# The last chunk of a mixture of experts: which engine adds products 1, 2 and 5 to the results

## The chip, the cores and the metric

The kernel runs on one core of one Trainium2 chip. The core's engines work side by side, each through its own queue in order, and wait for each other by semaphores: TensorE multiplies matrices into PSUM, VectorE and ScalarE work on tensors elementwise and can read PSUM, GpSimd works elementwise on SBUF, and SyncE (SP) issues DMAs, as ScalarE and GpSimd can too. The metric is the device time of one execution in microseconds (us). A profile is one further execution, recorded instruction by instruction.

## The reference

Two stages follow each other. The first is attention with two kinds of heads (4 batches, 8 heads, 768 positions, head size 64); its output is laid out as x with 3072 tokens of 512 values. The second is a mixture of 8 experts in which every expert works on every token:

```
logits = x @ w_gate
P = exp(logits - max);  8 times: P /= row sums, P /= column sums, P *= N / E
for e in range(8):
    h = max(x @ w1[e], 0)          # 3072 x 1024
    ye = h @ w2[e]                 # 3072 x 512
    out += P[:, e:e+1] * ye
```

Only the last `h @ w2[e]` and its weighted sum into `out` are touched here.

## The kernel before

The attention and the first expert come first and are not touched. Then a list `works` holds all pairs (e, c): experts 1 to 7, and for each the six chunks c of 512 tokens. The last pair is (7, 5).

Each of the two matrix products of a chunk is made by a scheme of the Strassen kind, with seven products of half-size blocks in place of eight and sums of blocks before and after. `left` and `right` (L611, L620) make the sums of input blocks on VectorE: two of the seven left factors of the second layer are plain blocks of h that serve products 1 and 2, one is a plain block for product 4, and four are sums. `combine_h` (L644) makes these four, in the order X[0] to X[3]: product 5 takes X[0], product 6 takes X[1] (which needs X[0]), product 7 takes X[2], and product 3 takes X[3] (which needs X[1]). Each is a sum over 128x1024 16-bit values at L617.

`layer2` (L734) multiplies. Its products accumulate in PSUM, in three groups called y, z and w, so that a product is added to what its bank already holds: y collects products 1, 6, 7, 4, w collects 5 and 3, z has product 2 alone. After each product the bank's present content belongs to one block (i, n) of the results, so it is read at once, and the next product of that group waits for the reader. `steps` (L771) lists group and block of each:

```
1: ("y", True, False, (0, 0)), 2: ("z", True, True, (0, 0)), 5: ("w", True, False, (1, 1)),
6: ("y", False, False, (0, 1)), 3: ("w", False, True, (0, 1)),
7: ("y", False, False, (1, 1)), 4: ("y", False, True, (1, 0)),
```

Each product has two halves q of 128x256. In the last chunk (`final`) each half has a PSUM bank of its own, so that TensorE can fill one while the other is read; in all other chunks both halves share a bank.

`add` (L754) reads the bank and adds it, times the token's weight for the expert (a column of Pne), to the result tile `acc[c]`. There are two ways. VectorE does it in one instruction per half (scalar_tensor_tensor, L764). Or ScalarE makes a scaled copy of both halves in a tile named add (L761, three buffers), and GpSimd issues a DMA that adds the tile to `acc[c]`, which lies in SBUF (L769). Products 2, 3 and 4 go the second way in all chunks but the last two, where VectorE adds everything. A block is stored (`store`, L727) when its last product of expert 7 has been added: block (0, 0) after products 1 and 2, (1, 1) after 5 and 7, (0, 1) after 6 and 3, (1, 0) after 4 alone. For the last chunk one half of each store is issued by SP and the other by ScalarE's queue.

What sets the order: `body` (L792) runs one pair, and in its seven slots interleaves the first layer of the next chunk with the second layer of the one before. After the last pair a loop runs the second layer of the last chunk alone, with the two remaining sums of h between its first steps (L822 to L824). VectorE's instructions stand in just the order in which this code issues them, as the whole loop is under a manual schedule for VectorE. The order on the other engines is left to a scheduler, which keeps the dependences and may move matmuls of one product between those of another. In the kernel before TensorE's order in the last chunk is 1, 5, 2 (but for one matmul), 6, the rest of 2, 3, 7, 4. VectorE's is: sums X[0], X[1], X[2], both adds of product 1, sum X[3], and then the adds of 5, 6, 2, 7, 3 and 4.

Of the kernel before, what the change touches and what calls it, by code (L numbers as in the profile page):

```python
# [14 lines left out]
ALU = mybir.AluOpType  # L15
# [17 lines left out]
def kernel(  # L33
# [13 lines left out]
    nc = tc.nc  # L47
# [28 lines left out]
    acc = [xp.tile([128, 2, 2, 2, 256], F32, tag=f"acc{c}", name=f"acc{c}") for c in range(NB // 4)]  # L76
# [79 lines left out]
    def round_first(h0):  # L156
# [9 lines left out]
        out=ret_u,  # L166
# [20 lines left out]
        out=retf, in_=ret_u.rearrange("p (e two) -> p e two", two=2)[:, :, 0]  # L187
# [140 lines left out]
    def first_steps(b, g):  # L328
# [18 lines left out]
        def layer2(sb):  # L347
# [10 lines left out]
            return 2  # L358

        return [partial(layer1, i) for i in range(4)], [partial(layer2, sb) for sb in range(2)]  # L360

    fillers = []
# [8 lines left out]
    with tc.manual_schedule(engines={mybir.EngineType.Pool}):  # L371
        nc.gpsimd.affine_select(
            out=ident16, in_=ident16, compare_op=ALU.is_equal, fill=0.0,
            base=0, pattern=[[-1, 128]], channel_multiplier=1,
        )
        for o in range(2):
# [3 lines left out]
                out=f4, in_=f4, compare_op=ALU.is_ge, fill=0.0,  # L380
# [4 lines left out]
                out=w4, in_=w4, compare_op=ALU.is_ge, fill=0.0,  # L385
# [187 lines left out]
    for it in range(8):  # L573
# [3 lines left out]
            out=Pne, in0=Pne, in1=rr.unsqueeze(2).broadcast_to([128, NB, E]), op=ALU.mult  # L577
        )
        nc.vector.tensor_reduce(
            out=bs, in_=Pne.transpose([0, 2, 1]), axis=AX.X, op=ALU.add  # L580
# [5 lines left out]
        if it == 7:  # L586
            nc.vector.tensor_scalar(
                out=rcs, in0=rcs, scalar1=float(NTOK) / E, scalar2=None, op0=ALU.mult
            )
        nc.vector.tensor_tensor(  # L590
            out=Pne, in0=Pne, in1=rcs.unsqueeze(1).broadcast_to([128, NB, E]), op=ALU.mult
# [16 lines left out]
    works = [(e, c) for e in range(1, E) for c in range(NCH)]  # L608
# [118 lines left out]
    def store(c, i, n):  # L727
        for o in range(2):
            (nc.scalar if c == NCH - 1 and o else nc.sync).dma_start(
                out=out[ts(c, CH), :].rearrange("(q i p c) (n d) -> i n c p q d", q=2, i=2, c=2, n=2)[i, n, o],  # L730
                in_=acc[c][64 * o:64 * o + 64, i, n, :, :],
            )

    def layer2(e, c):  # L734
        banks = {}
        final = (e, c) == works[-1]

        def product(k, bank, first, last=False):
            if first and final:
                banks[bank] = [psB.tile([128, 512], F32, tag="l1" if bank == "y" else "l2",  # L740
                                        name=f"l2{bank}{q}")[:, 0:256] for q in range(2)]
            elif first:
                t = psB.tile([128, 2, 256], F32, tag="l2", name=f"l2{bank}")
                banks[bank] = [t[:, q, :] for q in range(2)]
            for q in range(2):
                for f in range(4):
                    nc.tensor.matmul(  # L747
                        out=banks[bank][q], lhsT=lefts2[e, c][k - 1][:, q, f, :],
                        rhs=rights2[e][k - 1][:, f, :],
                        start=(first and (final or q == 0) and f == 0),  # L750
                        stop=(last and (final or q == 1) and f == 3), skip_group_check=True,
                    )

        def add(bank, i, n, by_dma):  # L754
            if by_dma:
                t = mp.tile([128, 2, 256], F32, tag="add", bufs=3, name="add")
            for q in range(2):
                dst = acc[c][:, i, n, q, :]
                w = Pne[:, 4 * c + 2 * q + i, e:e + 1]
                if by_dma:  # L760
                    nc.scalar.activation(out=t[:, q, :], in_=banks[bank][q], func=AF.Copy,  # L761
                                         bias=0.0, scale=w)
                else:
                    nc.vector.scalar_tensor_tensor(  # L764
                        out=dst, in0=banks[bank][q], scalar=w, in1=dst,
                        op0=ALU.mult, op1=ALU.add,
                    )
            if by_dma:
                nc.gpsimd.dma_start(out=acc[c][:, i, n, :, :], in_=t, accum_op=ALU.add)  # L769

        steps = {  # L771
            1: ("y", True, False, (0, 0)), 2: ("z", True, True, (0, 0)), 5: ("w", True, False, (1, 1)),
            6: ("y", False, False, (0, 1)), 3: ("w", False, True, (0, 1)),
            7: ("y", False, False, (1, 1)), 4: ("y", False, True, (1, 0)),
        }
        done = {}
        for k in (1, 5, 6, 2, 7, 3, 4):
            bank, first, last, (i, n) = steps[k]
            product(k, bank, first, last)
            add(bank, i, n, k in (2, 3, 4) and (e, c) not in works[-2:])  # L780
            done[i, n] = done.get((i, n), 0) + 1
            if e == E - 1 and done[i, n] == (1 if (i, n) == (1, 0) else 2):
                store(c, i, n)
            yield
# [7 lines left out]
    def body(n):  # L792
        e, c = works[n]
        if c == 0 and e + 1 < E:
            expw[e + 1] = load_expert(e + 1)
        if c == 2 and e + 1 < E:
            gens["w"] = combine_w(e + 1)
        if e == 1:
            gens["first"] = weight_first(c)
            gens["x"] = combine_x((c + 1) % NCH)  # L800
        for slot in range(7):
            go("l1", 2 if n == 0 and slot == 0 else 1)
            if slot in (1, 3):
                go("w")
                go("x", 2)
            go("l2")
            if slot in (2, 3, 5, 6):
                go("first")
            if slot in (2, 3):
                go("h")  # L810
            if n == 0 and slot == 0:
                run(combine_w(1), 9)
        gens["h"] = combine_h(e, c)
        go("h", 2)
        gens["l2"] = layer2(e, c)
        if n + 1 < len(works):
            gens["l1"] = layer1(*works[n + 1])
# [41 lines left out]
```

## Time and profile before

| | us |
|---|---|
| median of 6 runs | 706.03 |
| lowest and highest run | 705.28 and 706.4 |
| the profiled execution | 705.86 |
| its span from first to last recorded instruction | 704.1 |
| TensorE at work in the span | 686.2 |
| VectorE | 569.3 |
| ScalarE | 416.9 |
| GpSimd | 151.4 |
| first matmul of the last chunk's second layer | at 690.02 |
| last add of VectorE starts, lasts | at 698.64, 0.48 |

The program ends shortly after the span. In the tables below, times are counted from the span's start; a row such as `L764 DVE ... acc_84<-l2y_10647,Pne,acc_84` is an instruction of line 764 on VectorE (DVE) that writes acc_84, the results of the last chunk, and reads the PSUM bank of one half of group y. PE is TensorE, PEld its weight load, ACT ScalarE, POOL GpSimd, SP SyncE.

### The profile page before, as it was taken

The page shows a single profiled execution, that of the slowest core. Times are in us where ns is not written, and L with a number is a line of the kernel's source. Part 1 is how long each engine was busy: PE and PEld are TensorE (multiplying, and loading weights), DVE is VectorE, ACT ScalarE, POOL GpSimd, SP SyncE. Part 2 cuts the span into 40 slices and gives each one's busy share as a digit, 9 for nine tenths or more (in the row PEclk, how much of TensorE's full clock was granted, in tenths as well). Part 3 has the DMA queues.
Part 4 walks back from the last instruction along what each step waited for, and adds up shares of the span by engine and source line. Part 5 has one row for each costly group of instructions (what it writes and reads, how often), then busy time and mean ns, then how long its engine had stood idle before and what let it go on. Part 6 is the DMA issues. An engine that isn't in the chain of part 4 may idle for free.

```text
span 704.1 us, 17055 instructions
## 1 busy us (share of the span) xinstructions
PE 686.2 (97%) x6932; PEld 570.0 (81%) x6932; DVE 569.3 (81%) x1158; ACT 416.9 (59%) x779; POOL 151.4 (22%) x183
## 2 busy tenths in 40 slices
PE   7999999999999999999999999999999999999995
PEld 3666666666588888888888888888888888888884
DVE  6775765757889978898888879887888889877786
ACT  6787676774885555555555555555655555555550
POOL 7431220000012131212212121222212121121210
PEclk8999999999999999999999999999999999999999
DMA  9999591000734287346924694359424954345774
GB/s 179 180 191 129 47 79 15 2 1 3 118 61 76 47 133 122 62 75 110 145 48 77 95 145 76 61 82 163 84 48 76 151 90 76 61 76 111 149 160 122
DMA packets 84223, 65.61 MB, mean 93 GB/s; under 512 B 48304, under 2 KB 64688, under 8 KB 84144
## 3 DMA queue, kind: packets, MB, share of 16 engines
q0 software_dynamic: 74976, 57.17, 58.6%
q1 hardware_dynamic: 7536, 6.30, 3.6%
q10 hardware_dynamic: 1632, 1.05, 0.5%
q8 instruction: 54, 0.88, 0.5%
q14 instruction: 25, 0.20, 0.1%
HBM read 52.45 MB, written 6.29 MB: 83 GB/s over the span
## 4 chain that ended last, share of the span: by engine, by line
PE 61%; DVE 1%; issue 0%; ACT 0%; DVEq 0%
PE l1y L679 17%; PE l2y L747 17%; PE l1w L679 9%; PE l2w L747 9%; PE l2z L747 4%; PE l1z L679 4%; DVE acc_84 L764 1%; DVE S_7_5_10640 L617 0%; DVE S_7_5_10643 L617 0%; DVE S_7_5_10642 L617 0%; DVE acc_83 L764 0%; ACT R_4602 L688 0%; DVEq L854 0%; DVE S_7_5_10641 L617 0%
## 5 line engine op out<-in xcount | busy, mean ns | idle before, releaser
L761 ACT ACTIVATE add<-l2w,Pne 128x256 f32<-128x256 f32 x80 | 33.7, 473 | 66.3 <-PE l2w L747 64.1
L761 ACT ACTIVATE add<-l2y,Pne 128x256 f32<-128x256 f32 x80 | 33.8, 474 | 11.0 <-PE l2y L747 10.0
L761 ACT ACTIVATE add<-l2z,Pne 128x256 f32<-128x256 f32 x80 | 33.7, 473 | 8.7 <-PE l2z L747 8.7
L337 PEld LDWEIGHTS <-w_0_126 128*128 128x128 f16 x384 | 35.4, 98 | 4.1 <-issue 0.2
L769 POOL DMA_DIRECT2D acc_79<-add x21 | 17.7, 844 | 78.8 <-ACT add L761 57.7
L769 POOL DMA_DIRECT2D acc_82<-add x21 | 17.8, 847 | 68.0 <-ACT add L761 68.0
L769 POOL DMA_DIRECT2D acc_81<-add x21 | 17.7, 844 | 68.0 <-ACT add L761 68.0
L769 POOL DMA_DIRECT2D acc_80<-add x21 | 17.7, 845 | 67.9 <-ACT add L761 67.9
L769 POOL DMA_DIRECT2D acc_83<-add x18 | 15.1, 841 | 54.7 <-ACT add L761 46.8
L769 POOL DMA_DIRECT2D acc_84<-add x18 | 15.4, 854 | 44.5 <-ACT add L761 44.0
L764 DVE SCALAR_TENSOR_TENSOR acc_79<-l2y,Pne,acc_79 128x256 f32<-128x256 f32 x42 | 18.3, 477 | 7.2 <-PE l2y L747 7.1
L764 DVE SCALAR_TENSOR_TENSOR acc_83<-l2y,Pne,acc_83 128x256 f32<-128x256 f32 x44 | 19.1, 477 | 3.2 <-PE l2y L747 3.2
L764 DVE SCALAR_TENSOR_TENSOR acc_80<-l2y,Pne,acc_80 128x256 f32<-128x256 f32 x42 | 18.3, 477 | 4.1 <-PE l2y L747 4.1
L764 DVE SCALAR_TENSOR_TENSOR acc_82<-l2y,Pne,acc_82 128x256 f32<-128x256 f32 x42 | 18.3, 477 | 4.1 <-PE l2y L747 4.1
L764 DVE SCALAR_TENSOR_TENSOR acc_81<-l2y,Pne,acc_81 128x256 f32<-128x256 f32 x42 | 18.3, 477 | 4.1 <-PE l2y L747 4.1
L764 DVE SCALAR_TENSOR_TENSOR acc_84<-l2y,Pne,acc_84 128x256 f32<-128x256 f32 x36 | 15.7, 477 | 7.1 <-PE l2y L747 7.1
L679 PEld LDWEIGHTS <-S_2_3734 128*128 128x128 f16 x192 | 18.8, 98 | 2.7 <-issue 0.5
L679 PEld LDWEIGHTS <-S_5_6872 128*128 128x128 f16 x192 | 18.8, 98 | 2.2
L679 PEld LDWEIGHTS <-S_4_5838 128*128 128x128 f16 x192 | 18.8, 98 | 2.2
L679 PEld LDWEIGHTS <-S_6_7906 128*128 128x128 f16 x192 | 18.8, 98 | 2.2
L679 PEld LDWEIGHTS <-S_7_8940 128*128 128x128 f16 x192 | 18.8, 98 | 2.2
L679 PEld LDWEIGHTS <-S_3_4804 128*128 128x128 f16 x192 | 18.8, 98 | 2.2
(2581 smaller groups left out, 2260.3 us busy)
## 6 DMA issues: line engine op xcount, KB each, us to landing
acc_79<-add POOLq DMA_DIRECT2D x21, 256.0 KB, 3.4
acc_80<-add POOLq DMA_DIRECT2D x21, 256.0 KB, 3.3
acc_81<-add POOLq DMA_DIRECT2D x21, 256.0 KB, 3.3
acc_82<-add POOLq DMA_DIRECT2D x21, 256.0 KB, 3.3
acc_83<-add POOLq DMA_DIRECT2D x18, 256.0 KB, 3.4
acc_84<-add POOLq DMA_DIRECT2D x18, 256.0 KB, 9.8
w_0_126<-in_moe_w_dram POOLq DMA_DIRECT2D x1, 1024.0 KB, 11.5
w_0_133<-in_moe_w_dram POOLq DMA_DIRECT2D x1, 1024.0 KB, 18.2
```

The costliest lines, as they stand in the source:

```text
L337: nc.tensor.matmul(out=l1[:, ts(fb % 2, 256)], lhsT=w1[:, dc, ts(fb, 128)], rhs=xT[dc // 2][:, dc % 2, c0:c0 + 256], start=(dc == 0), stop ...
L679: nc.tensor.matmul(out=banks[g, bank][:, f, :], lhsT=lefts1[e][k - 1][:, dc, ts(2 * g + f, 128)], rhs=rights1[c][k - 1][:, dc, :], start=( ...
L747: nc.tensor.matmul(out=banks[bank][q], lhsT=lefts2[e, c][k - 1][:, q, f, :], rhs=rights2[e][k - 1][:, f, :], start=(first and (final or q ...
L761: nc.scalar.activation(out=t[:, q, :], in_=banks[bank][q], func=AF.Copy, bias=0.0, scale=w)
L764: nc.vector.scalar_tensor_tensor(out=dst, in0=banks[bank][q], scalar=w, in1=dst, op0=ALU.mult, op1=ALU.add,)
L769: nc.gpsimd.dma_start(out=acc[c][:, i, n, :, :], in_=t, accum_op=ALU.add)
```

## The change

In the last chunk alone, the products are issued in the order 1, 2, 5, 6, 7, 3, 4. Products 1, 2 and 5 go by ScalarE's scaled copy, and in place of the accumulating DMA GpSimd adds the copy to the results with one instruction over both halves (tensor_tensor, 128x512 f32). VectorE keeps the adds of products 6, 7, 3 and 4. In the last chunk but one VectorE still adds everything, and the other chunks stay as they were.

```diff
-            if by_dma:
+            if by_dma and final:
+                nc.gpsimd.tensor_tensor(out=acc[c][:, i, n, :, :], in0=t,
+                                        in1=acc[c][:, i, n, :, :], op=ALU.add)
+            elif by_dma:
                 nc.gpsimd.dma_start(out=acc[c][:, i, n, :, :], in_=t, accum_op=ALU.add)
...
-        for k in (1, 5, 6, 2, 7, 3, 4):
+        for k in (1, 2, 5, 6, 7, 3, 4) if final else (1, 5, 6, 2, 7, 3, 4):
             bank, first, last, (i, n) = steps[k]
             product(k, bank, first, last)
-            add(bank, i, n, k in (2, 3, 4) and (e, c) not in works[-2:])
+            add(bank, i, n, k in (1, 2, 5) if final else k in (2, 3, 4) and (e, c) != works[-2])
             done[i, n] = done.get((i, n), 0) + 1
```

After the change VectorE's order in the last chunk is: the four sums X[0] to X[3], then the adds of 6, 7, 3 and 4. TensorE's is 1, 2, 5, 6, two matmuls of 3, 7, the rest of 3, 4. GpSimd adds 1, 2 and 5 in this order; the add of 2 reads what that of 1 wrote, and VectorE's add of 7 reads what GpSimd's add of 5 wrote.

## The prediction

> Products are called P1 to P7 after the key of `steps`, the four sums of h u0 to u3 (S_7_5_10640 to S_7_5_10643 in the trace; P5 reads u0, P6 u1, P7 u2, P3 u3). Every product ends in two adds, one per half q. "The last chunk" is (7, 5).
>
> **What bounds the kernel now.** I read the page first: TensorE is busy for 97% of the span, so over most of the kernel a change to other engines is worth nothing.
>
> ```profile
> PE 686.2 (97%) x6932; PEld 570.0 (81%) x6932; DVE 569.3 (81%) x1158; ACT 416.9 (59%) x779; POOL 151.4 (22%) x183
> ```
>
> The change touches only the last chunk, so next come the busy times by stretch (engine busy times with their instruction counts, TensorE's granted clock, DMA share, GB/s) of the chunk's end and of what follows it.
>
> ```profile
> 690.00:699.20 9.20, 6.86 (x58) 5.29 (x56) 9.04 (x21) 0.00 (x0) 0.00 (x0) 1.00 0.39 94
> 699.20:704.10 4.90, 0.00 (x0) 0.00 (x0) 0.00 (x0) 0.00 (x0) 0.00 (x0) 0.68 0.53 162
> ```
>
> In the 9.20 us from 690.00 VectorE is busy for 9.04, TensorE for 6.86, ScalarE and GpSimd for nothing. VectorE bounds this stretch alone. Then 4.90 us pass with no engine at work: the last stores land and the program ends. That part follows VectorE's last add, whenever this comes.
>
> The chain of waits confirms it (start, length, what): from 691.10 on it is VectorE nearly without a break.
>
> ```profile
> 691.10 0.61 DVE S_7_5_10640 L617
> ...
> 692.35 0.53 DVE S_7_5_10642 L617
> ...
> 692.95 0.87 DVE acc_84 L764 x2
> 693.82 0.60 DVE S_7_5_10643 L617
> ...
> 695.12 1.29 DVE acc_84 L764 x4
> ...
> 697.08 1.65 DVE acc_84 L764 x4
> 698.73 0.39 DVEq L854
> ```
>
> The timeline (start, duration, engine, line) gives the prices. Eighteen VectorE instructions, 4 sums and 14 adds, fill 691.02 to 699.12.
>
> ```profile
> 690.02 0.60 PE L747 MATMUL l2y_10647<-w_7_8560,hT_5_10474 128*128 128x256 f16 x4
> 690.46 0.60 PE L747 MATMUL l2y_10648<-w_7_8560,hT_5_10474 128*128 128x256 f16 x4
> 691.02 0.68 DVE L617 TENSOR_TENSOR S_7_5_10640<-hT_5_10474 128x1024 f16<-128x1024 f16 x1
> 691.74 0.69 DVE L617 TENSOR_TENSOR S_7_5_10641<-S_7_5_10640,hT_5_10474 128x1024 f16<-128x1024 f16 x1
> ...
> 696.68 0.48 DVE L764 SCALAR_TENSOR_TENSOR acc_84<-l2y_10647,Pne,acc_84 128x256 f32<-128x256 f32 x1
> ...
> 697.08 0.48 DVE L764 SCALAR_TENSOR_TENSOR acc_84<-l2y_10648,Pne,acc_84 128x256 f32<-128x256 f32 x1
> 697.21 0.60 PE L747 MATMUL l2y_10647<-T_7_9285,hT_5_10474 128*128 128x256 f16 x4 [0.44 <-DVE acc_84 L764]
> ...
> 698.64 0.48 DVE L764 SCALAR_TENSOR_TENSOR acc_84<-l2y_10648,Pne,acc_84 128x256 f32<-128x256 f32 x1
> ```
>
> Read from these: a sum lasts 0.68 and the next can start 0.61 after it, or 0.72 where it reads the one before (691.02 to 691.74). An add lasts 0.48 with the next 0.39 behind it. Half a product takes TensorE 0.44 (690.02 to 690.46), its last result 0.60 after its first matmul. An add's end lets TensorE back into its bank 0.05 later (697.16 to 697.21).
>
> [...]
>
> **The change part by part.**
>
> Removed: six adds of VectorE (P1, P2, P5), 6 x 0.39 = 2.34 us of the engine that bounds the stretch. With u3 moved in front of all adds, the sums go at 691.02, 691.74, 692.35, 692.96, and u3 ends at 693.64.
>
> Reordered on TensorE: P2 goes before P5. P1 and P2 need only h, so TensorE works at 690.90 to 691.77 where it now waits 0.70 for u0. P5 is issued from 691.78 (u0 ends at 691.70), P6 from 692.65 (u1 ends at 692.43). In the scheduled order two matmuls of P3's first half stand before P7, the other six behind it, then P4; so u3 must be there before P7 starts, and it is (693.64 against 694.1).
>
> Added on ScalarE: six scaled copies. L761 shows 0.47 each, 0.84 per pair (678.00 in the trace). ScalarE has nothing else to do after 689.95, so these cost nothing but latency: pairs end at 691.55, 692.43 and about 693.3. The stores on ScalarE's queue stand behind them and need later data anyhow. If that cover went, P6 would feel it first: its first half is done at 693.25 and its add, behind the sums, starts at 693.56, so 0.3 us are to spare.
>
> Added on GpSimd: three adds of 128x512 f32, d each. [...] The fixed part I take from this trace's affine selects: 289 ns for 128 elements, 418 ns for 256, so 1.0 ns an element and 0.16 fixed. [...] The add of P2 also waits for that of P1, which it reads: 0.1 more. GpSimd's own queue has nothing else left; its last accumulating DMA was issued at 679.13.
>
> The wait that is added: VectorE's first add of P7 goes to block (1,1), after GpSimd's add of P5 to it. VectorE runs in order, so the other add of P7, both of P3 and both of P4 queue behind, and P4's matmuls wait too, since they go into the y banks that P7's adds read. Call T5 the end of GpSimd's third add.
>
> Without that wait: P6's adds at 693.56 and 693.95; P7's halves at 694.09 and 694.53; P7's adds at 694.73 and 695.17, P3's at 695.56 and 695.95, P4's at 696.34 and 696.73, end 697.21. That is 1.9 below 699.12, the most that can be gained.
>
> With it, if T5 is late: 0.07 to start, five steps of 0.39, one 0.48, so the end is T5 + 2.5. P4's halves fit in (ready 1.15 and 1.6 after P7's first add starts; wanted at 1.56 and 1.95). The gain is gone at T5 = 696.6.
>
> T5 under the lock: [...] If GpSimd comes last, T5 = 693.64 + 0.1 + 3 x 1.27 + 0.1 = 697.65. It is nearly the same when GpSimd's first add slips in at 691.70 between u0 and u1: u1 to u3 then run together behind it, and two adds are left. So the end is 700.15, 1.0 later than now. [...] I choose this case: [...].
>
> The stores keep their order; each last pair is issued as P4's adds end. SP's four issues take 0.60 each and are spaced as widely as before, so the 4.9 us behind the last add stay. The profiled execution took 705.86 with a span of 704.1; it becomes 705.86 + 1.0 = 706.9. It lies 0.17 under the median of the runs, 706.03, for which 707.0 follows.
>
> **The rivals.**
>
> No lock in effect: GpSimd's adds run beside the sums, T5 = 691.60 + 3.81 + 0.1 = 695.5, end 698.0, 1.1 gained: 704.9. [...] 1.9 is the limit: 704.1. For it: the trace of before shows no blocking of one engine by the other anywhere. [...]
>
> Slower: [...] P5's copy is there at 693.3; once P1's add has pushed u1 back to 693, P2's and P5's adds can stand ahead of u3, the latter without a semaphore between them. Then u3 ends at 691.02 + 2.62 + 3.81 + 0.3 = 697.75, and behind u3 in VectorE's order stand all eight adds, 3.57 to the end as in the free case: 701.3, 2.2 later, 708.2. It decides as soon as all three GpSimd adds go before u3; with only two before it, the end is T5's again. [...] Against: u1 to u3 leave no gap between them.
>
> A first-use or completion cost of GpSimd's add that I don't price would delay T5 directly, [...]: over 707.4. The trace speaks against much: GpSimd's first affine select took 289 ns.
>
> **How the numbers follow.** About 0.2%, 1.4 us, is what a measurement of this kernel tells from no change. Lock with GpSimd last 0.52 (706.5 to 707.5, of it 0.06 beyond 1.4); no lock 0.28 (704.1 to 705.4, of it 0.13 beyond 1.4); u3 behind GpSimd 0.15; unpriced GpSimd cost 0.05, nearly all slower. So faster 0.13, slower 0.06 + 0.15 + 0.04 = 0.25, same 0.62. The forecast is 707.0, no change that can be told. The range 704.6 to 708.0 leaves out the best of the second case and most of the third and fourth.
>
> **What would show it.** Right: the sums keep 0.61 to 0.72 between them or have one break of about 1.3 us, GpSimd's adds fall outside them, VectorE stands idle for some 3 us before P7's first add with GpSimd as releaser, and the last add ends near 700. Wrong: GpSimd's adds overlapping the sums at full pace, or P7's add waiting for TensorE alone (no lock, or d under 1); [...] a start-to-start spacing of GpSimd's adds away from 1.3; ScalarE's copies or TensorE's P6 late.

## The result, and the profile after

The change makes the kernel slower: 707.88 us median (10 runs, 707.53 to 708.48) against 705.61 for the kernel before on the same chip (20 runs, 704.81 to 706.74). The ratio is 1.0031, with a 95% interval of 1.0022 to 1.0039; that is 2.2 us, of which the interval allows 1.6 to 2.8. The profiled execution took 708.92 us with a span of 707.2, more than any of the ten.

The page shows what was moved: VectorE has six instructions fewer and is nevertheless busy for longer (569.3 us before), and GpSimd has three more.

```profile
PE 687.9 (97%) x6932; PEld 570.8 (81%) x6932; DVE 570.7 (81%) x1152; ACT 419.7 (59%) x785; POOL 156.1 (22%) x186
```

The timeline of the changed kernel (start, duration, engine, line, then in brackets the idle time before and who ended it) shows where VectorE's time went.

```profile
691.72 0.68 DVE L617 TENSOR_TENSOR S_7_5_10640<-hT_5_10474 128x1024 f16<-128x1024 f16 x1
...
692.42 4.61 POOL L769 TENSOR_TENSOR acc_84<-add,acc_84 128x512 f32<-128x512 f32 x3 [11.74 <-ACT add L761]
692.44 1.80 DVE L617 TENSOR_TENSOR S_7_5_10641<-S_7_5_10640,hT_5_10474 128x1024 f16<-128x1024 f16 x1
...
694.17 1.75 DVE L617 TENSOR_TENSOR S_7_5_10642<-hT_5_10474 128x1024 f16<-128x1024 f16 x1
...
695.84 1.75 DVE L617 TENSOR_TENSOR S_7_5_10643<-hT_5_10474,S_7_5_10641 128x1024 f16<-128x1024 f16 x1
...
697.64 0.60 PE L747 MATMUL l2w_10678<-w_7_8560,S_7_5_10643 128*128 128x256 f16 x2 [2.29 <-DVE S_7_5_10643 L617]
...
698.03 1.06 PE L747 MATMUL l2y_10647<-T_7_9285,S_7_5_10642 128*128 128x256 f16 x4
...
699.20 0.48 DVE L764 SCALAR_TENSOR_TENSOR acc_84<-l2y_10647,Pne,acc_84 128x256 f32<-128x256 f32 x1 [0.83 <-PE l2y_10647 L747]
...
702.14 0.48 DVE L764 SCALAR_TENSOR_TENSOR acc_84<-l2y_10648,Pne,acc_84 128x256 f32<-128x256 f32 x1
```

The sum u0, with GpSimd idle, still takes 0.68 us. The three sums beside GpSimd's adds take 1.75 to 1.80, for the work that took 0.68 to 0.69 each in the kernel before. Some 1.1 us of each recorded duration is thus time in which the sum is held up: VectorE looks busy while it waits, and no list of waits shows this. u3 ends at 697.59, 5.87 us after u0's start (2.62 had been expected for sums alone). All of VectorE's eight adds stand behind it. P7's product needs only u2, which is done at 695.92, but on TensorE two matmuls of P3 stand before it, and they need u3.

Then a second thing happens. A half product takes 1.06 us from its first matmul to its last result at 698.03; in the kernel before it takes 0.60. The busy times by stretch show TensorE's granted clock in the third column from the right (before it: busy time and number of instructions of PE, PEld, DVE, ACT, POOL).

```profile
695.30:697.60 2.30, 0.04 (x1) 0.00 (x0) 2.30 (x3) 0.00 (x0) 1.74 (x2) 1.00 0.37 89
697.60:698.00 0.40, 0.36 (x2) 0.27 (x3) 0.40 (x2) 0.00 (x0) 0.00 (x0) 0.62 0.42 144
698.00:700.80 2.80, 2.80 (x15) 1.97 (x13) 1.67 (x4) 0.00 (x0) 0.00 (x0) 0.50 0.00 0
700.80:702.60 1.80, 1.30 (x10) 0.88 (x8) 1.43 (x4) 0.00 (x0) 0.00 (x0) 0.91 0.38 83
```

TensorE has nothing to do from 695.35 to 697.64, as it waits for u3. Just after it starts again its granted clock is 0.50, against 1.00 in the first row: for all 2.80 us of the third row and, by an estimate from the means of 0.62 and 0.91, for about 0.3 us in each of the rows beside it, 3.4 us in all. In this stretch it is TensorE that VectorE waits for, as the chain of waits (start, length, what) says too:

```profile
692.44 1.80 DVE S_7_5_10641 L617
...
695.84 1.76 DVE S_7_5_10643 L617
...
698.24 0.85 PE l2y_10647 L747 x4
699.09 0.85 PE l2y_10648 L747 x4
...
701.70 0.92 DVE acc_84 L764 x2
```

From the chunk's first matmul to the end of VectorE's last add it is 11.89 us (690.73 to 702.62), 9.10 in the kernel before (690.02 to 699.12). That is 2.79 more. The rest of the span, 4.58 us, is 0.40 shorter. The first matmul itself comes 0.71 later in this execution, with no instruction changed ahead of it; the profiled executions of all kernels here differ by up to 1.2 us in this, so the distances from that matmul are compared below, and the times by their medians. 2.79 - 0.40 = 2.39 fits the 2.2 us of the ratio.

### The profile page after: what moved, and what is told of

Same layout as the page of the kernel before. It is cut to its first block, busy times and chain, and to the rows that moved or that the text cites. A ratio compares the mean times of both kernels' runs of the same rounds, so it can differ in the third digit from the quotient of the medians.

```text
span 707.2 us, 17062 instructions
## 1 busy us (share of the span) xinstructions
PE 687.9 (97%) x6932; PEld 570.8 (81%) x6932; DVE 570.7 (81%) x1152; ACT 419.7 (59%) x785; POOL 156.1 (22%) x186
## 3 DMA queue, kind: packets, MB, share of 16 engines
q10 hardware_dynamic: 1632, 1.05, 0.5%
## 4 chain that ended last, share of the span: by engine, by line
PE 61%; DVE 1%; issue 0%; ACT 0%
PE l1y L679 17%; PE l2y L747 17%; PE l1w L679 9%; PE l2w L747 9%; PE l2z L747 4%; PE l1z L679 4%; DVE S_7_5_10641 L617 0%; DVE S_7_5_10643 L617 0%; PE l2y_10647 L747 0%; PE l2w_10678 L747 0%; DVE acc_84 L764 0%; PE l2w_10679 L747 0%; PE l2y_10648 L747 0%; DVE S_7_5_10640 L617 0%; DVE acc_83 L764 0%
```

## The experiments

The theory: GpSimd's adds and the sums of h take turns, which delays u3 (the port theory; what the two share, no run shows); the wait for u3 is what makes TensorE's clock fall to the 0.50 seen behind it (the clock theory). Rivals: the new order of products; ScalarE's copies, which write SBUF at the same time; P7's wait for GpSimd's add of P5.

All kernels in one table. "Sums" is from u0's start to u3's end, "adds" from the chunk's first matmul to the end of VectorE's last add, both in us in one profiled execution; the ratio to the kernel before is over all runs.

| kernel | sums | adds | ratio and interval |
|---|---|---|---|
| before | 3.39, P1's adds among them | 9.10 | |
| the change | 5.87 | 11.89 | 1.0031 (1.0022 to 1.0039) |
| e1_order | 3.39, P1's adds among them | 11.06 | 1.0005 (0.9998 to 1.0011) |
| e2_two | 4.79 | 10.23 | 1.0014 (1.0006 to 1.0023) |
| e3_gate | 2.62 | 10.20 | 1.0009 (1.0003 to 1.0016) |
| e4_gate5 | 2.61 | 7.64 | 1.0012 (1.0006 to 1.0019) |
| e5_warm | 5.87 | 10.60 | 1.0017 (1.0010 to 1.0024) |
| e6_memset | 2.60 | 7.18 | 0.9983 (0.9976 to 0.9990) |
| e7_direct | none | 7.67 | 0.9976 (0.9966 to 0.9986) |
| e8_stores | 2.60 | 7.64 | 0.9989 (0.9983 to 0.9996) |
| e9_after | 5.86 | 11.81 | 1.0033 (1.0022 to 1.0045) |
| e10_warm | 5.86 | 10.61 | 1.0022 (1.0015 to 1.0029) |

**The order alone (e1_order).**

```diff
-            add(bank, i, n, k in (1, 2, 5) if final else k in (2, 3, 4) and (e, c) != works[-2])
+            add(bank, i, n, not final and k in (2, 3, 4) and (e, c) != works[-2])
```

> The last chunk's products in the new order 1, 2, 5, 6, 7, 3, 4, but all fourteen adds on VectorE as before; no scaled copies, no GpSimd adds. Port theory (GpSimd's adds and the sums of h take turns [...], and that alone delays the sums): the sums keep 0.6 to 0.72 us between them, VectorE has its 18 instructions in a row again, and the time is that of before within 0.3 us. Rival (the new order itself, with the sums and TensorE's products placed otherwise, costs the time): 1 to 2 us of the 2.3 us loss stay.

Between 0.1 us less and 0.8 us more than before: the order doesn't carry the loss of 2.2 us, though a part of up to 0.8 us isn't ruled out. The sums are back at 0.68 to 0.69 us. The profiled execution took 707.8, far above this kernel's median of 706.25, and in it TensorE's clock fell to 0.50 behind two gaps of 0.67 and 1.14 us; its 11.06 us are therefore not typical.

**GpSimd kept off the sums (e3_gate).** GpSimd's three adds are held back in a list `pending`. A copy of one column of u3 stands before them, and they follow in the order P1, P2, P5.

```diff
...
+            if final and k == 5:
+                gate = mp.tile([128, 1], F16, tag="gate", bufs=1, name="gate")
+                nc.gpsimd.tensor_copy(out=gate, in_=lefts2[e, c][2][:, 0, 0, 0:1])
+                for key in sorted(pending, key=lambda x: x[2]):
+                    pending[key]()
+                store(c, 0, 0)
...
```

> The changed kernel, but GpSimd first copies one column of u3, so that its three adds start only when all four sums are done. Port theory: sums at 0.6 to 0.72 us again, u3 done 2.6 us after u0 starts (5.9 in the changed kernel), GpSimd's adds 1.27 us each with nothing in their way, so T5 about 4.3 us after u3 and the last add 2.5 us after T5: 1.3 us slower than before, up to 1.8 if TensorE's clock falls while P4 waits. Rival (the sums were slowed by ScalarE's copies, which write SBUF at the same time): sums stay well over 1 us, as the copies have not moved, and the time is 3 us or more over before.

The timeline of this kernel (names without numbers):

```profile
692.52 0.69 DVE L617 TENSOR_TENSOR S<-S,hT 128x1024 f16<-128x1024 f16 x1
...
693.19 0.91 ACT L761 ACTIVATE add<-l2w,Pne 128x256 f32<-128x256 f32 x2
...
693.73 0.69 DVE L617 TENSOR_TENSOR S<-hT,S 128x1024 f16<-128x1024 f16 x1
...
694.71 3.82 POOL L790 TENSOR_TENSOR acc<-add,acc 128x512 f32<-128x512 f32 x3
...
698.56 0.88 DVE L764 SCALAR_TENSOR_TENSOR acc<-l2y,Pne,acc 128x256 f32<-128x256 f32 x2 [3.36 <-POOL acc L790]
```

The sums keep their pace, 0.68 to 0.69 us, while ScalarE's copies run beside them, so the copies are not what slowed them. Now the wait that the prediction priced is the bound: VectorE stands 3.36 us until GpSimd's third add is done. The time came out 0.6 us over before (interval 0.2 to 1.1), less than the 1.3 to 1.8 expected; the adds end 1.10 later in the profile, and TensorE's granted clock is 1.00 up to the end of its gap of 2.54 us (the mean from 696.0 to 699.1), with 1.03 us for the product behind it, as for P7 ahead of it.

**P7's wait taken away, and one GpSimd add with it (e2_two).**

```diff
-            add(bank, i, n, k in (1, 2, 5) if final else k in (2, 3, 4) and (e, c) != works[-2])
+            add(bank, i, n, k in (1, 2) if final else k in (2, 3, 4) and (e, c) != works[-2])
```

> The changed kernel, but P5's adds are VectorE's again; GpSimd adds P1 and P2 only, with nothing to hold them back. Port theory with turns taken: two GpSimd adds of 1.27 us come among the sums in place of three, so u3 is done about 1.4 us earlier than in the changed kernel, 4.5 us after u0 starts; two more VectorE adds stand behind it: 0.6 to 1.6 us over before. Rival (P7's wait for GpSimd's add of P5 costs the time): with that wait gone VectorE runs free, and the time falls to or below that of before.

The timeline:

```profile
691.76 1.80 DVE L617 TENSOR_TENSOR S<-S,hT 128x1024 f16<-128x1024 f16 x1
...
693.49 1.75 DVE L617 TENSOR_TENSOR S<-hT 128x1024 f16<-128x1024 f16 x1
...
695.16 0.68 DVE L617 TENSOR_TENSOR S<-hT,S 128x1024 f16<-128x1024 f16 x1
...
696.29 1.03 PE L747 MATMUL l2w<-w,S 128*128 128x256 f16 x8 [1.62 <-DVE acc L764]
```

1.0 us over before (0.4 to 1.6), as the port theory has it: u1 and u2, beside GpSimd's two adds, take 1.80 and 1.75 us, and u3, with nothing beside it, 0.68. One add less makes the sums 1.08 us shorter. VectorE no longer waits for GpSimd at all, and the kernel is still not as fast as before: the rival falls. TensorE stood idle for 0.78 and then 1.62 us here, but its products behind these gaps took 1.03 to 1.05 us each, with a mean granted clock of 0.998 over the execution, so this loss is not the clock's.

**TensorE kept at work (e5_warm, then e10_warm beside e9_after).**

```diff
             product(k, bank, first, last)
+            if final and k == 6:
+                t = psB.tile([128, 512], F32, tag="l1", name="warmb")
+                for r in range(24):
+                    nc.tensor.matmul(out=t[:, 0:256], lhsT=lefts2[e, c][5][:, r % 2, 0, :],
+                                     rhs=rights2[e][5][:, 0, :], start=True, stop=True)
```

> The changed kernel with 24 extra matmuls of 128x256 behind P6, into a PSUM bank that nobody reads, so that TensorE does not stand idle while it waits for u3. Clock theory (the 2.3 us without work halved TensorE's granted clock, and the products behind u3 at half speed cost about 1.4 us): four matmuls take 0.60 us instead of 1.06 behind u3, the granted clock stays at 1.0 there, and the time is 0.8 to 1.3 us over before instead of 2.3. Rival (VectorE's queue behind u3 is what ends last, whatever TensorE's clock): no gain, 2.3 to 2.6 over before.

It ran a second time, beside the changed kernel itself:

> The changed kernel once more, beside the one with extra matmuls on the same chip. Port theory and clock theory: 2.0 to 2.6 us over before; u1 to u3 take 1.75 to 1.8 us each again in the profile. If the fall of TensorE's clock depends on when the gap comes, the four matmuls behind u3 may take 0.60 or 1.06 us in this profile.

> The kernel with 24 extra matmuls behind P6 once more, on the same chip as the changed kernel. Clock theory: 0.6 to 1.4 us faster than the changed kernel beside it, its four matmuls behind u3 at 0.60 us. Rival (no clock effect): the same time as the changed kernel within 0.4 us.

The first row is from the timeline, the second from the busy times by stretch of the second of these runs.

```profile
694.85 2.78 PE L786 MATMUL warmb<-T,S 128*128 128x256 f16 x24
...
697.70 1.03 PE L747 MATMUL l2y<-T,S 128*128 128x256 f16 x8
```

```profile
698.00:701.00 3.00, 2.48 (x23) 1.96 (x21) 2.63 (x7) 0.00 (x0) 0.00 (x0) 1.00 0.12 26
```

A whole product takes 1.03 us again and the clock stays at 1.00. In the changed kernel's second profile the clock fell as in the first:

```profile
698.00:700.80 2.80, 2.80 (x14) 1.97 (x14) 1.66 (x5) 0.00 (x0) 0.00 (x0) 0.50 0.01 3
```

The adds end 1.20 us earlier with the extra matmuls (10.61 against 11.81), and the medians differ by 0.90 (707.46 and 708.36). In the separate runs the ratios to the kernel before, 1.0017 and 1.0031, differ by 1.0 us. The intervals of each pair of ratios overlap a little, so I take about 0.9 us as likely, not as fixed to a tenth. The sums stay at 5.86 us: the clock is the second, smaller part of the loss.

**GpSimd writing but not reading (e6_memset).**

```diff
-                nc.gpsimd.tensor_tensor(out=acc[c][:, i, n, :, :], in0=t,
-                                        in1=acc[c][:, i, n, :, :], op=ALU.add)
+                nc.gpsimd.memset(t, 0.0)
```

> GpSimd's three adds replaced by a fill of the copy tile with zeros, behind the same waits: products 1, 2 and 5 are left out of the results. Port theory in the form that only a GpSimd instruction that reads SBUF blocks the sums: sums at 0.6 to 0.72 us, no wait before P7's add, 1.5 to 1.9 us faster than before. Rival ([...]): each sum behind one is longer by the fill's own 0.5 us or so, and 0.5 to 1.5 us of the gain are lost.

The timeline:

```profile
692.88 0.53 POOL L769 MEMSET add<- 128x512 f32 x1 [11.71 <-ACT add L761]
692.93 0.69 DVE L617 TENSOR_TENSOR S<-S,hT 128x1024 f16<-128x1024 f16 x1
...
693.70 0.53 POOL L769 MEMSET add<- 128x512 f32 x1 [0.29 <-ACT add L761]
...
694.14 0.68 DVE L617 TENSOR_TENSOR S<-hT,S 128x1024 f16<-128x1024 f16 x1
```

The fills, 0.53 us each, lie right over the sums, and the sums still take 0.68 to 0.69: the rival, that an instruction of GpSimd which only writes holds them up too, falls. The adds differ from the fills in that they read two tensors in SBUF, and in their 1.27 us; which of the two counts, no run here tells. The adds end 1.92 us earlier than before, which is the 1.9 that the prediction called the most that can be gained; the time gained 1.2 (0.7 to 1.7), somewhat less than the 1.5 to 1.9 expected.

**P5 first behind u3 (e4_gate5, then e8_stores).**

```diff
-                for key in sorted(pending, key=lambda x: x[2]):
+                for key in sorted(pending, key=lambda x: (x[:2] == (0, 0), x[2])):
                     pending[key]()
-                store(c, 0, 0)
...
+                if final and k == 4:
+                    store(c, 0, 0)
```

> As the kernel in which GpSimd waits for u3, but GpSimd adds P5 first and P1 and P2 after it, and block (0, 0) is stored last. Port theory: the sums stay at 0.6 to 0.72 us; P7's first add starts 1.7 us after u3's end (4.2 in the kernel with P5 last, 1.1 with no wait); VectorE's last add and GpSimd's last both end some 4.1 us after u3: 0.8 to 1.3 us faster than before. Rival (GpSimd's adds also hold up VectorE's adds from PSUM that run beside them): those adds take more than 0.48 us each, and less than 0.5 us is gained.

A miss that teaches something. VectorE's part went as expected, P7's first add starts 1.6 us behind u3, the adds end 1.46 us earlier than before, and VectorE's adds keep 0.87 to 0.88 us a pair beside GpSimd's, so the rival of this run falls; and the kernel is 0.8 us slower (0.4 to 1.3). The program's order of the stores is not the queue's: the scheduler put the store of (0, 0), which waits for GpSimd's last add, first in both queues. The first row below is from the timeline (ScalarE's queue issues its four stores from 697.81 on), the others from the busy times by stretch, where the next-to-last column is the DMA share.

```profile
697.81 2.94 ACTq L729 DMA_DIRECT2D out_dram<-acc  x4
```

```profile
694.00:696.00 2.00, 2.00 (x18) 1.56 (x17) 1.20 (x4) 0.00 (x0) 2.00 (x2) 1.00 0.00 0
696.00:697.00 1.00, 0.81 (x8) 0.48 (x5) 1.00 (x4) 0.00 (x0) 0.92 (x2) 1.00 0.00 0
697.00:698.00 1.00, 0.00 (x0) 0.00 (x0) 0.68 (x2) 0.00 (x0) 0.78 (x1) 1.00 0.00 0
...
699.00:702.00 3.00, 0.00 (x0) 0.00 (x0) 0.00 (x0) 0.00 (x0) 0.00 (x0) 0.83 0.92 267
```

No store moves from 694 to 698, though block (1, 1) is done at 696.1, and then all eight stand in line. With the queues' order written out:

```diff
-        with tc.manual_schedule(engines={mybir.EngineType.DVE, mybir.EngineType.Pool}):
+        with tc.manual_schedule(engines={mybir.EngineType.DVE, mybir.EngineType.Pool,
+                                         mybir.EngineType.SP, mybir.EngineType.Activation}):
```

> As the kernel with P5 first behind u3, but SP's and ScalarE's queues issue the stores in the order in which the blocks are done: (1, 1), (0, 1), (1, 0), and (0, 0) last. There the store of (0, 0), which waits for GpSimd's last add, stood first in both queues, so that all eight issues came after 697.8. If that was what took the gain (its VectorE adds ended 7.6 us after the first matmul, 9.1 in before): 1.0 to 1.5 us faster than before. Rival (something else behind the last add, or TensorE's clock, took it): within 0.4 us of the kernel before, or slower.

The timeline:

```profile
693.93 3.83 POOL L790 TENSOR_TENSOR acc<-add,acc 128x512 f32<-128x512 f32 x3
...
696.18 3.06 ACTq L729 DMA_DIRECT2D out_dram<-acc  x4
```

The adds end just as early, the stores go out from 696.18 on, and the kernel is 0.8 us faster than before (0.3 to 1.2): 1.6 us between two kernels whose engines do the same. It gained less than expected: the last store is issued at 698.5, against 699.2 in the kernel before. GpSimd's third add is done at 697.76 and doesn't hold it up; the four issues of the queue follow each other closely from 696.18 on and fill 3.06 us. This version of the change, with the same engines for the same adds, beats the kernel before.

**Without sums (e7_direct).** If VectorE bounds the end, the saved eighth product is bought too dearly there:

```diff
+    def layer2_direct(e, c):
+        h, w2 = hTs[e, c], expw[e][1]
+        for i in range(2):
+            for n in range(2):
+                for q in range(2):
+                    t = psB.tile([128, 512], F32, tag="l2", name="l2d")[:, 0:256]
+                    for f in range(8):
+                        nc.tensor.matmul(out=t, lhsT=h[:, q, f, ts(i, 128)], rhs=w2[:, f, ts(n, 256)],
+                                         start=(f == 0), stop=(f == 7))
...
+                store(c, i, n)
```

> Made from the kernel before: the last chunk's second layer as eight plain products, each block's two accumulated in PSUM; no sums of h, eight VectorE adds in place of fourteen, nothing on ScalarE and GpSimd. If VectorE and not TensorE bounded the end of before: TensorE becomes the bound with 64 matmuls of 0.109 us and no wait, the last add ends 7.7 us after the first matmul (9.1 in before), 1.0 to 1.5 us faster than before, and the granted clock stays at 1.0. Rival (the Strassen scheme's saved product is worth what it costs here too, as TensorE is the busiest engine of the page): 0.5 us slower to no change.

The timeline:

```profile
690.06 7.15 PE L793 MATMUL l2d<-w,hT 128*128 128x256 f16 x64
...
697.25 0.48 DVE L796 SCALAR_TENSOR_TENSOR acc<-l2d,Pne,acc 128x256 f32<-128x256 f32 x1 [0.39 <-PE l2d L793]
```

TensorE works without a break and VectorE waits for it, 0.39 us at each add but the first. The adds end 7.67 us after the first matmul, 7.7 had been worked out, and the kernel is 1.7 us faster than before (1.0 to 2.4), median 704.29. It has the lowest ratio of the kernels here (its interval overlaps a little with those of e6_memset and e8_stores), and the chunk's end needs neither ScalarE nor GpSimd.

## Why the prediction was right, and where it was not

The number held: 707.0 was forecast with 704.6 to 708.0, and 707.88 lies at the range's upper edge, on the slower side, where 0.25 stood. The likeliest case was not the one that happened. That the number held is in part luck of the base: 708.0 is 2.0 above the 706.03 from which the forecast was counted, and the change cost 2.2 against 705.61. From 706.03 that would be 708.2, outside the range. The forecast was also for no change that can be told, with 1.4 us as the measure, and the loss is clear of that (1.6 to 2.8).

- What bounds the end: right. With VectorE's work really made shorter (e6_memset, e7_direct, e8_stores) the end moves.
- ScalarE's copies and TensorE's new order cost nothing: right for the copies (e3_gate). The order alone shows nothing beyond 0.8 us (e1_order).
- GpSimd's add at d = 1.27, an estimate of mine that the trace of before does not show: right. Its first add took 1.27, and three in a row with no sum beside them 3.82 (e3_gate).
- The lock, my assumption that a sum of h and an add of GpSimd don't run side by side: right in the changed kernel, where a sum took 0.68 us alone and 1.75 to 1.80 beside an add; beside a fill that only writes it took 0.68 to 0.69 (e6_memset). The trace of before has no add of GpSimd and showed nothing of it, so the weight of 0.52 was an estimate of mine. A sum and an add are not kept apart for their full recorded times: a turn of the two takes 1.67 us and not 0.61 + 1.27.
- The step that failed is "T5 under the lock": "If GpSimd comes last" took for granted that u1 to u3, with no gap between them, run in a row. They don't: the engines take turns, one add, one sum, and all three adds go before u3. The turns follow the order of the recorded starts: the adds start at 692.42, 693.8 and 695.3, u1 to u3 at 692.44, 694.17 and 695.84. A sum's start is recorded 0.07 to 0.08 us before the end of the sum ahead of it, and the start of GpSimd's next add is recorded before that. So P7's add never waited for GpSimd; it waited for its own product, and the product for u3. That P7's add waits for TensorE alone is a sign that the prediction had named for being wrong. This is the slower rival, to which I gave 0.15 with "u1 to u3 leave no gap between them" against it.
- That rival's 2.2 us are close to the measured 2.2 by errors that nearly cancel. Its u3 ended 7.73 us after the first matmul, measured 6.86: a turn takes 1.67 us (u2 ends at 695.92, u3 at 697.59), not 0.61 + 1.27 + 0.1. Behind u3 it had 3.57 us, measured 5.03: TensorE's halved clock was in no case of mine. And the end behind the last add came out 0.40 shorter than before. Some 1.2 of the 1.46 behind u3 come back in the profile when TensorE is kept at work, and some 0.9 in the medians.
- The end behind the last add stays at 4.9: it is 4.58 (4.98 in the kernel before by the same count), close enough here. As a rule it failed in e4_gate5, where a store at the head of a queue cost more than all the adds had gained.

What stays open: the exact share of TensorE's clock in the 2.2 us, and what makes it fall; the fall itself is seen in profiled executions alone. Not tried is the changed kernel with P7 wholly before P3 on TensorE. By an estimate from e8_stores, where 2.45 us pass from P7's first add to the end of the last, P7's adds right behind P6's (697.51 + 0.78), with the clock at 1.00, would let the adds end near 700.7 in place of 702.62.

## What to carry to other kernels

Before work leaves a busy VectorE for GpSimd, look at what VectorE runs just then. Here the sums of two SBUF tensors took 1.75 to 1.80 us beside GpSimd's adds in place of 0.68 (the changed kernel), while VectorE's adds from PSUM took 0.87 to 0.88 a pair beside them, as without them (e4_gate5; 0.87 in the kernel before). Where two instructions meet that the trace shows taking turns, put GpSimd's behind VectorE's (e8_stores, 0.8 us faster than before) or price one full turn per pair, 1.67 us here. A late producer can cost twice: u3 kept TensorE waiting for 2.29 us in the changed kernel, and the granted clock of 0.50 behind that wait cost some 0.9 us more by the medians of e9_after and e10_warm; behind a gap of 2.54 us in e3_gate there was no such cost. And before an overloaded end is spread over more engines, ask whether the scheme that loads it still pays there: the plain product came out with the lowest ratio, 0.9976, of all that was tried.

## What the runs showed of the hardware

- VectorE's sums and GpSimd's adds alternate where both are queued, even where VectorE's next sum (u2) waits for nothing else; 1.67 us a turn in the changed kernel, where the two take 0.61 and 1.27 us apart. The lost time is recorded as busy time of both: the sums are recorded with 1.75 to 1.80 us in place of 0.68, GpSimd's second and third add with 1.59 and 1.71 in place of 1.27.
- TensorE's granted clock fell to 0.50 for about 3.4 us behind gaps of 0.79 and 2.29 us with one product between them in the changed kernel's profile, and again to 0.50 behind the same gaps in its second one (e9_after), and behind 0.67 and 1.14 us with one product between them in e1_order's. Behind 0.78 and 1.62 us with one product between them the next two products took 1.03 and 1.04 us (e2_two), and behind a single gap of 2.54 us the next took 1.03 (e3_gate); at 0.50 a product took 1.91 us (e9_after). The length of the gaps alone doesn't decide it.
